# Second batch's scores and norms placed behind the first unit's products in an attention and MLP kernel

## The chip, the cores and the metric

One core of one Trainium2 chip runs the whole kernel. The metric is the device time of one execution in microseconds (us). Three runs of the kernel before took 824.13, 827.89 and 828.71 us; the median is 827.89 us.

## What is computed

The reference takes q, k and v of 4 batches, 8 heads, 576 positions and 64 features, and chains three blocks:

```python
out_up    = repeat(softmax_attention(mean4(q), mean4(k), mean4(v)), 4)   # 144 pooled positions
out_local = softmax(where(|i - j| < 4, q k^T / 8, -1e9)) v               # banded attention
x  = out_up + out_local                     # to (4, 576, 512)
u  = x + real(fft(fft(x, axis=1), axis=2))
ch = relu(layernorm(u) @ w_ch1) @ w_ch2     # 512 -> 2048 -> 512
y  = u + ch
out = (sigmoid(causal_conv5(y)) * (y @ w_val)) @ w_out
```

All inputs and outputs are float32. The weights reach the core as 64-bit floats and are turned into 32-bit ones by three integer operations on VectorE (DVE).

## The kernel before

The work has three kinds. **Attention and transform of a batch** (`attn_steps(b)`, L367): banded scores in five windows (`scores`, tile dS; then softmax into dP; `values`, tiles dPT, PT, dO), pooled attention (`lowres`, tiles sc, E, eT, po), then the transform: folds fs and fF, their fp16 halves FH and FL (L695 to L714), a first product over features (ab, L729) and a second over positions (pp, pq, pn, L754), added into X. **Twelve units** of 192 positions, three for each batch, `mlp_steps` (L907): layer norm `ln(b, j)` (L804, tiles uc, sq, st), eight groups of first products (`h_group`, tile ph), eight groups of second products (`c_group`, tile pc). Unit (0, 0) runs in 32-bit on the raw weights (`steps32`, L872, lines L885 and L896); the eleven others in three fp16 passes (L920, L938), for which the weights must first be split in halves (`conv_w`, L318). **The closing block** of a unit, `moe2_steps` (L961): taps of the convolution, `val` (L1017), `out_tile` (L1033). It needs the last weights, w_val and w_out (`weights3_steps`, L1095).

Weights arrive by `load_w(i)` (i = 0 to 7 the first matrix, 8 to 15 the second). `word_w(i)` (L283) makes 32-bit words of one slice, three DVE operations of 1024 columns, or twice three of 512 where the raw slice sits in two small buffers. `sumsq_w(i)` (L299) adds the squares of the slice on TensorE (PE, tile gram), and `w2_scale` takes the scale of the halves from that.

The order is set in two ways. Each step is put at a position on a line of time (`put`, `spread`; one unit is 1.0, unit n runs from n to n + 1, the start is negative) by the constants S_.. and P_.. at the head of the file; the steps are emitted in order of position. The framework then orders each engine's instructions when the kernel is built, by emission order, by priorities (`urgent`) and by its own model of the times; on the chip every engine runs its list in order. Two things bend this by hand: `behind(gate, f)` (L250) lets f's instructions be issued only after the gate instruction on the same engine, and the lists `gates` and `gates2` hold DVE instructions behind which the three operations of the weight words are placed, one entry for each operation until the last is left (L283 to L289). `load` chains the input transfers on SyncE's queue (SP) one behind the other in emission order until position S_CH = 0.9.

In the start, each word step of the second matrix is followed by its sum of squares (`w_in2`, S_W2 = -7.4 to -6.9); `ln(0, 0)` is put at S_N0 = -7.5, `ln(0, 1)` at S_N1 = -6.85, the second batch's scores at P_D[1] = -6.4 to -3.8. The first unit's products are put at 0 to 1. The scores of the second batch's first three windows use the two banks ps_h, which the first products use too (D1_H = 3).

Of the kernel before, what the change touches and what calls it, by code (L numbers as in the profile page):

```python
# [36 lines left out]
NSQ = 8  # L37
P_TAIL = ((0.08, 0.2), (-0.03, 0.03), (0.3, 0.5))
NORM_V = ((1, 0), (1, 1))
LN_V = ((0, 0), (1, 0), (2, 0), (3, 0))  # L40
CHAIN = True
S_CH = 0.9
S_LD = (-12.14, -11.9)
# [10 lines left out]
S_N0 = -7.5  # L54
S_W2 = (-7.4, -6.9)
S_C2 = (0.89, 0.94)
S_W3 = (0.945, 1.3)
P_D = {1: (-6.4, -3.8), 2: (1.6, 3.2), 3: (4.4, 6.0)}
P_E = {1: (0.2, 1.2), 2: (3.3, 4.5), 3: (6.1, 7.4)}
P_L = {1: 1.8, 2: 4.9, 3: 7.8}  # L60
EN_G = (1,)
SUM_V = (0,)
LN_PE = ((0, 0), (0, 1))
S_N1 = -6.85
XB_G = ((1, 1), (1, 3))
LASTV = True
U = {'F': 3000, 'N': 3000, 'X': 600, 'M': 0, 'V': 1000, 'O': 0, 'W': 0, 'R': 2000, 'S': 4000}
# [1 line left out]
P_VAL = (0.38, 0.65)  # L69
P_OUT = (1.12, 1.75)  # L70
P_LN = 0.3
D1_H = 3
LN_H = ()
LR0 = 0
TURN_V = False
# [42 lines left out]
def attn_moe_kernel(ctx, tc, qk_t, v_t, w1, w2, w_val, conv_t, w_out, c_feat, c_seq, c_band, c_eye, c_pool, out):  # L118
# [246 lines left out]
    st = {}  # L365

    def attn_steps(b):  # L367
# [60 lines left out]
        def dense(sp):  # L428
# [34 lines left out]
            def scores(r, e):  # L463

                q0, nq = QWIN[r]
                m = sc["band"][:, min(r, 1)].unsqueeze(1).to_broadcast([P, 4, P])
                pss = []
                for par in range(2):
                    ps = ps_h.tile([P, 4, P], F32, tag="h", name="dS") if first or (b == 1 and r < D1_H) else pst("dS", [P, 4, P])
                    behind(st[0]["seqed"].ins if b == 1 and r == 0 and par == 0 else None, lambda: T.matmul(  # L470
                        out=ps[0:nq], lhsT=sc["band"][:, 2, 0:nq], rhs=m, start=True, stop=False))
                    pss.append(ps)
                for a in range(4):
                    for par in range(2):
                        row = slice(par * 64, par * 64 + 64)
                        T.matmul(out=pss[par][0:nq, a], lhsT=d["X"][row, a, PAD + q0:PAD + q0 + nq],  # L476
                                 rhs=kT[a // 2][row, a % 2, WIN[r]:WIN[r] + 128], start=False, stop=(a == 3))
                mx = tiny.tile([P, 2, 4], F32, tag="dmx", name="dmx")
                su = tiny.tile([P, 2, 4], F32, tag="dsu", name="dsu")
                for par in range(2):  # L480
                    i = V.tensor_reduce(out=mx[0:nq, par], in_=pss[par][0:nq], axis=AX.X, op=ALU.max)  # L481
                if first:
                    gates.extend([i.ins] * (3 if r else 2))
                A.activation(out=mx[0:nq], in_=mx[0:nq], func=AF.Copy, scale=-SCALE)
                for par in range(2):
                    if first:
                        s_ = sp.tile([P, 4, P], F32, tag="S", name="dP", bufs=NS)
                    else:
                        s_ = mainp["S"].tile([P, 4, P], F32, tag="S", name="dP1")
                    for a in range(4):  # L490
                        to = {} if b in SUM_V else {"accum_out": su[0:nq, par, a:a + 1]}
                        A.activation(out=s_[0:nq, a], in_=pss[par][0:nq, a], func=AF.Exp, scale=SCALE,  # L492
                                     bias=mx[0:nq, par, a:a + 1], **to)
                    if b in SUM_V:
                        V.tensor_reduce(out=su[0:nq, par], in_=s_[0:nq], axis=AX.X, op=ALU.add)
                    e["s", par] = s_
                V.tensor_scalar(out=su[0:nq], in0=su[0:nq], scalar1=1e-9, scalar2=None, op0=ALU.add)
                V.reciprocal(out=su[0:nq], in_=su[0:nq])  # L498
                for par in range(2):
                    s_ = e["s", par][0:nq]  # L500
                    mul(V if b == 0 or (b, par) in NORM_V else G, s_, s_, su[0:nq, par].unsqueeze(2).to_broadcast([nq, 4, P]))
# [32 lines left out]
            if first:  # L534
                cuts = (0, WIN[2] + 128, S)
                ld = [lambda c=c, z=z, f=f: f(z, c, cuts[cuts.index(c) + 1])
                      for c in cuts[:2] for z in range(2) for f in (load_k, load_q)]
                for r in range(5):
                    ld.append(lambda r=r: load_vw(r))
                d["loads"] = [(1.0, f) for f in ld]  # L540
                for z in range(2):
                    for w in range(2):
                        steps.append((0.3, lambda z=z, w=w: pool_qk(z, w)))
                steps.append((0.3, lambda: pooled_v0(vw)))
            else:
                for z in range(2):
                    steps.append((0.1, lambda z=z: [load_k(z, 0, S), load_q(z, 0, S)]))
                steps.append((0.1, lambda: [load_vw(r) for r in range(5)]))

                def pool_v4(n):  # L550
                    x = [pr_t("v4", [QC, 512]) for _ in range(2)]
                    kc, h = n // 2, n % 2
                    for r in range(2):
                        load(out=x[r].rearrange("p (r c) -> p r c", r=2),
                             in_=v4[b, kc * QC:(kc + 1) * QC, 2 * r:2 * r + 2, h * 256:h * 256 + 256])
                    pooled_v([(kc, x)], n, h * 4, 4)
                v1 = [(0.1, lambda n=n: pool_v4(n)) for n in range(4)]
                for z in range(2):
                    for w in range(2):
                        steps.append((0.1, lambda z=z, w=w: pool_qk(z, w)))  # L560
            lr = []
            d["turned"] = len(steps)
            if b == 0:
# [129 lines left out]
        for sd in range(2):  # L693
            for c in range(2):
                def f(c=c, sd=sd):  # L695
                    X = d["X"]
                    s = prp.tile([P, S + 1], F32, tag="E", name="fs", bufs=3)
                    (V, V if b == 0 else G)[sd].tensor_tensor(
                        out=s, in0=X[:, c, PAD:PAD + S + 1], in1=X[:, c + 2, PAD:PAD + S + 1],
                        op=(ALU.add, ALU.subtract)[sd])  # L700
                    if b == 0:
                        F = mainp["tap"].tile([P, 2, HALF], F32, tag="tap", name="fF")
                    else:
                        F = prp.tile([P, 2, HALF], F32, tag="E", name="fF", bufs=3)
                    for e in range(2):
                        V.tensor_tensor(  # L706
                            out=F[:, e], in0=s[:, 0:HALF], in1=s[:, S:S - HALF:-1],
                            op=(ALU.add, ALU.subtract)[e])
                    h_ = d["FH"][:, c, sd, :, 0:HALF]
                    A.activation(out=h_, in_=F, func=AF.Copy, scale=d["sx"][:, 0:1])  # L710
                    i = stt(V, d["FL"][:, c, sd, :, 0:HALF], F, d["sx"][:, 0:1], h_, ALU.mult, ALU.subtract)
                    if b == 0:
                        gates2.extend([i.ins] * 2)
                steps.append((2.1, f))  # L714

        @step(0.0)
# [87 lines left out]
    def ln(b, j):  # L804
# [5 lines left out]
        def colsum(t, src):  # L810
            if (b, j) in LN_PE:
                ps = pst("st", [P, UT])
                for c in range(4):
                    T.matmul(out=ps, lhsT=ones, rhs=src[:, c], start=(c == 0), stop=(c == 3))
                return ps
            add(eng, t[:, 0:2], src[:, 0:2], src[:, 2:4])
            add(eng, t[:, 0], t[:, 0], t[:, 1])
            ps = ps_h.tile([P, UT], F32, tag="h", name="st") if (b, j) in LN_H else pst("st", [P, UT])
            T.matmul(out=ps, lhsT=ones, rhs=t[:, 0], start=True, stop=True)
            return ps  # L820
# [51 lines left out]
    def steps32():  # L872
# [4 lines left out]
        def h_group(g):  # L877
# [3 lines left out]
            for e in range(2):  # L881
                m = 2 * g + e
                for kc in range(4):
                    o = (m % 8) * 128
                    T.matmul(out=ps[:, e], lhsT=W[kc * 2 + m // 8 + 1][:, o:o + 128], rhs=u()[:, kc, :],  # L885
                             start=(kc == 0), stop=(kc == 3))
            A.activation(out=hs[-1][:, g % 2], in_=ps, func=AF.Relu)

        def c_group(g):
# [193 lines left out]
    def w_in2(i):  # L1083
        if i >= 11:
            load_w(i)
        w_in(i)

    def w_in(i):
        word_w(i)
# [36 lines left out]
    put(S_L1, lambda: [load_w(i) for i in range(8)])  # L1126
    put(S_K, load_consts2)
    put(S_W1[1], lambda: urgent(w1_scale, "S"))
    put(S_W2[1], lambda: urgent(w2_scale, "S"))
    put(S_LW2, lambda: [load_w(i) for i in range(8, 11)])  # L1130
    put(S_CH, lambda: chain.update(on=False))
    for steps, p in ((st[0]["loads"], S_LD), (a0[:c0], S_T0), (a0[c0:c1], S_S0), (a0[c1:], S_F0)):
# [26 lines left out]
    for n, (b, j) in enumerate(units):  # L1159
        main = mlp_steps(b, j)  # L1160
        spread([(1.0, f) for f in main], n, n + 1)
        if j + 1 < UPB:
            put(n + P_LN if n else S_N1, lambda b=b, j=j: urgent(lambda: ln(b, j + 1), "N"))
        ps = [P_TAP, P_VAL, P_OUT]
        if n == B * UPB - 2:
            ps[1:] = [tuple(1 + x for x in P_TAIL[1]), tuple(1 + x for x in P_TAIL[2])]
        if n == B * UPB - 1:
# [52 lines left out]
```

## Time and profile before

| | |
|---|---|
| Median of 3 runs | 827.89 us (824.13 to 828.71) |
| The profiled execution's own time | 826.63 us |
| Its span in the trace | 824.8 us |
| PE busy | 753.9 us (91%) |
| Weight loads into PE (PEld) busy | 651.7 us (79%) |
| DVE busy | 481.0 us (58%) |
| ScalarE (ACT) busy | 397.4 us (48%) |
| GpSimd (POOL) busy | 189.1 us (23%) |
| Granted PE clock, mean | 0.935 of 2.4 GHz |
| Read and written in HBM | 45.37 MB and 9.45 MB |

Times in the profile are from the start of the span. A tile's name without its number names all its buffers: W is any slice of the weights, X a batch's activations. A busy PE is not PE at its peak: matmuls overlap, so the pace is read from the distance between starts. The granted clock is 1.0 at 2.4 GHz and 0.5 at 1.2 GHz.

### The profile page before, as it was taken

How to read it: one execution, taken by the hardware profiler on the slowest of the kernel's cores; microseconds unless marked ns; L12 is line 12 of the kernel's file. 1: busy time of each engine (PE TensorE's matmuls, PEld its weight loads, DVE VectorE, ACT ScalarE, POOL GpSimd, SP SyncE). 2: the span in 40 equal slices, each digit the busy share in tenths (PEclk: the TensorE clock that was granted, in tenths of full speed). 3: DMA queues.
4: the chain of work that ended last, by engine and by line, in shares of the span. 5: the costliest groups of instructions: out<-in, count | busy, mean ns of one | idle time of the engine just before them, and what ended most of it. 6: DMA issues, size and time to landing. Idle time of an engine off the chain costs nothing.

```text
span 824.8 us, 17392 instructions
## 1 busy us (share of the span) xinstructions
PE 753.9 (91%) x7234; PEld 651.7 (79%) x7234; DVE 481.0 (58%) x942; ACT 397.4 (48%) x1156; POOL 189.1 (23%) x192
## 2 busy tenths in 40 slices
PE   5887687998979999998989999989989999999996
PEld 2666555887869898886869888978779998989894
DVE  5895968657878575336596732237765526252224
ACT  2573222545674366776562664575552516151512
POOL 0000000015243124363061341341232305040300
PEclk9875666899989999998999999999999999999998
DMA  9753540244202100122021000010110000000001
GB/s 323 312 188 127 182 149 0 86 128 146 77 2 87 59 16 26 35 80 81 29 72 59 1 15 22 9 43 2 53 59 4 14 1 14 14 15 2 26 2 39
DMA packets 25849, 53.58 MB, mean 65 GB/s; under 512 B 1989, under 2 KB 11973, under 8 KB 24746
## 3 DMA queue, kind: packets, MB, share of 16 engines
q1 hardware_dynamic: 25770, 52.47, 18.8%
q8 instruction: 57, 0.93, 0.5%
q14 instruction: 22, 0.18, 0.1%
HBM read 45.37 MB, written 9.45 MB: 66 GB/s over the span
## 4 chain that ended last, share of the span: by engine, by line
PE 65%; DVE 19%; DMA 5%; issue 4%; ACT 4%; POOL 3%; SPq 1%; POOLq 0%; DVEq 0%; ACTq 0%
PE pc L938 18%; PE ph L920 17%; PE val L1017 5%; PE out L1033 4%; DVE W L155 4%; PE dS L476 4%; DVE fF L706 2%; PE dO L522 2%; DVE FL L155 2%; PE ab L729 2%; PE po L650 2%; DMA v<-in_v_dram 2%; PE dPT L511 1%; DMA raw<-in_moe_w_val_dram 1%; DMA raw<-in_moe_w_out_dram 1%
## 5 line engine op out<-in xcount | busy, mean ns | idle before, releaser
L938 PE MATMUL pc<-hh,W 128*128 128x192 f16 x1408 | 199.1, 249 | 1.7 <-ACT hh L924 1.7
L920 PE MATMUL ph<-uh,W 128*128 128x192 f16 x1408 | 195.9, 247 | 0.3 <-ACT uh L849 0.3
L938 PEld LDWEIGHTS <-W 128*128 128x128 f16 x2112 | 178.4, 99 | 16.2 <-issue 11.2
L920 PEld LDWEIGHTS <-W 128*128 128x128 f16 x2112 | 176.0, 98 | 9.0 <-issue 5.7
L938 PE MATMUL pc<-hl,W 128*128 128x192 f16 x704 | 173.8, 250 | 4.3 <-DVE hl L155 4.3
L920 PE MATMUL ph<-ul,W 128*128 128x192 f16 x704 | 173.7, 247 | 1.4 <-DVE ul L850 1.4
L155 DVE SCALAR_TENSOR_TENSOR hl<-ph,hh 128x384 f16<-128x384 f32 x88 | 48.4, 552 | 116.9 <-ACT hh L924 116.9
L161 POOL TENSOR_TENSOR W<-W,tap 128x768 f32<-128x768 f32 x40 | 73.3, 1833 | 164.1 <-ACT tap L996 159.9
L924 ACT ACTIVATE hh<-ph 128x384 f16<-128x384 f32 x88 | 42.2, 484 | 80.7 <-PE ph L920 80.3
L996 ACT ACTIVATE tap<-X,cw 128x192 f32<-128x192 f32 x180 | 66.5, 445 | 8.2 <-DMA out_dram<-osb 4.8
L492 ACT ACTIVATE dP<-dS,dmx 112x128 f32<-112x128 f32 (+2 forms) x160 | 53.2, 372 | 10.2 <-PE dPT L511 9.8
L1017 PE MATMUL val<-yy,W 128*128 128x192 f16 x576 | 54.4, 249 | 2.0 <-DVE yy L155 1.2
L1017 PEld LDWEIGHTS <-W 128*128 128x128 f16 x576 | 49.0, 99 | 5.1 <-issue 3.6
L1033 PE MATMUL out<-W,gh 128*128 128x512 f16 x144 | 46.6, 383 | 0.0
L158 POOL TENSOR_TENSOR dP<-dP,dsu 112x512 f32<-112x512 f32 (+2 forms) x20 | 22.5, 1148 | 72.1 <-DVE dsu L498 57.8
L481 DVE TENSOR_REDUCE dmx<-dS 112x4 f32<-112x512 f32 (+2 forms) x40 | 27.2, 684 | 16.5 <-PE dS L476 16.2
L1033 PE MATMUL out<-W,gl 128*128 128x512 f16 x72 | 27.6, 383 | 2.1 <-DVE gl L155 2.1
L729 PE MATMUL ab<-feat,FH 128*97 128x128 f16 (+5 forms) x192 | 22.0, 244 | 8.1 <-ACT FH L710 7.8
L155 DVE SCALAR_TENSOR_TENSOR W<-W,W 128x1024 int32<-128x1024 int32 x24 | 28.6, 1214 | 0.0
L516 ACT ACTIVATE PT<-dPT 128x448 f32<-128x448 f32 (+2 forms) x40 | 21.7, 558 | 13.3 <-PE dPT L511 13.3
L729 PE MATMUL ab<-feat,FL 128*97 128x128 f16 (+5 forms) x96 | 18.3, 248 | 10.1 <-DVE FL L155 10.0
L511 PE MATMUL dPT<-eye,dP 112*128 112x112 f32 (+2 forms) x160 | 25.2, 294 | 1.6 <-ACT base L654 1.6
(207 smaller groups left out, 1357.8 us busy)
## 6 DMA issues: line engine op xcount, KB each, us to landing
W<-in_moe_w_ch_dram SPq DMA_DIRECT2D x12, 1024.0 KB
X<-in_qk_dram SPq DMA_DIRECT2D x8, 576.0 KB
out_dram<-osb SPq DMA_DIRECT2D x18, 256.0 KB
v<-in_v_dram SPq DMA_DIRECT2D x24, 144.0 KB
vwkv<-in_v_dram SPq DMA_DIRECT2D x12, 256.0 KB
dx<-X SPq DMA_DIRECT2D x4, 576.0 KB
dr<-dx SPq DMA_DIRECT2D x4, 576.0 KB
X<-dr SPq DMA_DIRECT2D x4, 576.0 KB
```

What stands on the lines that cost most here:

```text
L155: return eng.scalar_tensor_tensor(out=out, in0=in0, scalar=scalar, in1=in1, op0=op0, op1=op1)
L161: return eng.tensor_tensor(out=out, in0=a, in1=b, op=ALU.add)
L476: T.matmul(out=pss[par][0:nq, a], lhsT=d["X"][row, a, PAD + q0:PAD + q0 + nq], rhs=kT[a // 2][row, a % 2, WIN[r]:WIN[r] + 128], start=Fals ...
L492: A.activation(out=s_[0:nq, a], in_=pss[par][0:nq, a], func=AF.Exp, scale=SCALE, bias=mx[0:nq, par, a:a + 1], **to)
L511: T.transpose(out=ps[:, a, 0:nq], in_=e["s", par][0:nq, a], identity=eye[0:nq, 0:nq])
L729: T.matmul(out=ps[0:n, c0:c1], lhsT=d[x][:, c, sd, e, n0:n0 + n], rhs=feat[:, w, c, c0:c1], start=(t == 0), stop=(t == 5),)
L920: T.matmul(out=ps[:, e], lhsT=w1_ap(pw, kc, 2 * g + e), rhs=uh[px][:, kc, :], start=(t == 0), stop=(t == 11))
L924: A.activation(out=h_, in_=ps, func=AF.Relu)
L938: T.matmul(out=ps[m // 2][:, m % 2], lhsT=w2_ap(pw, kk, m), rhs=x[px][:, e, :], start=(kk == 0 and (pw, px) == (0, 0) and m % 2 == 0), sto ...
L996: A.activation(out=g[:, c], in_=X[:, c, c0:c0 + UT], func=AF.Copy, scale=cw[:, c, t:t + 1])
L1017: T.matmul(out=ps[:, e], lhsT=wv_ap(pw, kc, 2 * mh + e), rhs=m_["y"][px][:, kc, :], start=(t == 0), stop=(t == 11))
L1033: T.matmul(out=ps, lhsT=(gh, gl)[px][:, kc, t * 128:(t + 1) * 128], rhs=wo_ap(pw, kc), start=(n == 0), stop=(n == 11))
```

## The change

It moves steps on the line of time, and changes what some of them wait for.

- The word steps of the second matrix no longer carry their sums of squares; those are put at 0.2 to 0.44, and `w2_scale` at 0.44.
- `gates2` loses the eight entries of the transform's folds (FL). Left are six of the first product's halves (AL), four of the second's (DS), and the first norm (u).
- The scores of the second batch move from -6.4..-3.8 to 0.02..0.94, with their loads of v; those of the first window, and the sums of `ln(0, 1)`, are placed behind `ph`, the last matmul of the first unit's first group. They use the banks t, no longer ps_h. The pooling of k goes behind the scores.
- `ln(0, 1)` moves to 0.1, `ln(0, 2)` from 1.3 to 0.9, its adds from POOL to DVE.
- The second batch's pooled attention and transform move from 0.2..1.2 to 0.96..1.85, its first norm from 1.8 to 2.1; the third batch's scores begin at 2.0 instead of 1.6.
- The last weights move from 0.945..1.3 to 1.02..1.6; the first unit's taps from 0.95..1.35 to 1.4..1.75, its val from 1.38..1.65 to 1.8..2.0, its out from 2.12..2.75 to 2.3..2.75.

```diff
-LN_V = ((0, 0), (1, 0), (2, 0), (3, 0))
+LN_V = ((0, 0), (0, 2), (1, 0), (2, 0), (3, 0))
...
-S_W3 = (0.945, 1.3)
-P_D = {1: (-6.4, -3.8), 2: (1.6, 3.2), 3: (4.4, 6.0)}
-P_E = {1: (0.2, 1.2), 2: (3.3, 4.5), 3: (6.1, 7.4)}
-P_L = {1: 1.8, 2: 4.9, 3: 7.8}
+S_W3 = (1.02, 1.6)
+S_G2 = (0.2, 0.44)
+P_D = {1: (0.02, 0.94), 2: (2.0, 3.2), 3: (4.4, 6.0)}
+P_E = {1: (0.96, 1.85), 2: (3.3, 4.5), 3: (6.1, 7.4)}
+P_L = {1: 2.1, 2: 4.9, 3: 7.8}
+P_T0 = ((0.4, 0.75), (0.8, 1.0), (1.3, 1.75))
...
-S_N1 = -6.85
+S_N1 = 0.1
+S_N2 = 0.9
...
-D1_H = 3
+D1_H = 0
...
-                    behind(st[0]["seqed"].ins if b == 1 and r == 0 and par == 0 else None, lambda: T.matmul(
+                    behind(st[0]["ph"].ins if b == 1 and r == 0 else None, lambda: T.matmul(
...
-                    for w in range(2):
+                    for w in range(1 if b == 1 else 2):
                         steps.append((0.1, lambda z=z, w=w: pool_qk(z, w)))
+                if b == 1:
+                    v1 += [(0.1, lambda z=z: pool_qk(z, 1)) for z in range(2)]
...
                     i = stt(V, d["FL"][:, c, sd, :, 0:HALF], F, d["sx"][:, 0:1], h_, ALU.mult, ALU.subtract)
-                    if b == 0:
-                        gates2.extend([i.ins] * 2)
...
-                    T.matmul(out=ps, lhsT=ones, rhs=src[:, c], start=(c == 0), stop=(c == 3))
+                    behind(st[0]["ph"].ins if j else None, lambda c=c: T.matmul(
+                        out=ps, lhsT=ones, rhs=src[:, c], start=(c == 0), stop=(c == 3)))
...
+            if g == 0:
+                st[0]["ph"] = i
             A.activation(out=hs[-1][:, g % 2], in_=ps, func=AF.Relu)
...
     def w_in2(i):
         if i >= 11:
             load_w(i)
-        w_in(i)
+        word_w(i)
...
-    put(S_W2[1], lambda: urgent(w2_scale, "S"))
+    spread([(1.0, lambda i=i: sumsq_w(i, "w2", i == 8, i == 15)) for i in range(8, 16)], *S_G2)
+    put(S_G2[1], lambda: urgent(w2_scale, "S"))
...
-            put(n + P_LN if n else S_N1, lambda b=b, j=j: urgent(lambda: ln(b, j + 1), "N"))
+            put((n + P_LN if n > 1 else S_N2) if n else S_N1, lambda b=b, j=j: urgent(lambda: ln(b, j + 1), "N"))
         ps = [P_TAP, P_VAL, P_OUT]
+        if n == 0:
+            ps = list(P_T0)
```

## Rows read from the trace of the kernel before

**Rows 1.** The page, span in 40 slices of 20.6 us: PE busy, granted clock

```profile
PE   5887687998979999998989999989989999999996
...
PEclk9875666899989999998999999999999999999998
```

**Rows 2.** Timeline, all engines, 75 to 125 us: start, length, instruction

```profile
86.18 0.69 DVE L261 TENSOR_SCALAR W<-W 128x1024 int32<-128x1024 int32 x1
...
89.59 2.35 DVE L155 SCALAR_TENSOR_TENSOR W<-W,W 128x1024 int32<-128x1024 int32 x2
...
91.86 0.82 DVE L155 SCALAR_TENSOR_TENSOR FL<-fF,s_x,FH 128x578 f16<-128x578 f32 x1
```

**Rows 3.** Timeline, 105 to 147 us

```profile
107.97 1.06 PE L306 MATMUL gram<-W 128*128 128x128 bf16 x8
...
112.70 1.22 DVE L155 SCALAR_TENSOR_TENSOR W<-W,W 128x1024 int32<-128x1024 int32 x1
113.83 1.56 DVE L161 TENSOR_TENSOR X<-X,DS 128x289 f32<-128x289 f32 x4
...
123.72 2.93 PE L814 MATMUL st<-sq,ones 128*128 128x192 f32 x8
...
128.73 0.95 DVE L824 TENSOR_TENSOR uc<-X,st 128x768 f32<-128x768 f32 x1
...
131.24 0.96 DVE L158 TENSOR_TENSOR u<-uc,r 128x768 f32<-128x768 f32 x1
...
132.23 0.84 ACT L826 ACTIVATE sq<-uc 128x768 f32<-128x768 f32 x1 [5.93 <-DVE u L158]
...
133.99 5.13 DVE L529 TENSOR_REDUCE qkT<-X 128x288 f32<-128x1152 f32 x4
...
143.56 1.76 SPq L176 DMA_DIRECT2D vwkv<-in_v_dram  x4
...
145.92 1.04 PE L306 MATMUL gram<-W 128*128 128x128 bf16 x8 [1.12 <-DVE W L155]
```

**Rows 4.** Timeline of PE, 146.6 to 161 us

```profile
146.75 5.09 PE L885 MATMUL ph<-u,W 128*128 128x192 f32 x16
...
153.66 2.87 PE L885 MATMUL ph<-u,W 128*128 128x192 f32 x16 [0.58 <-ACT h L887]
...
157.16 0.40 PE L470 MATMUL dS<-bandb 128*112 128x512 bf16 x1
...
158.54 0.99 PE L522 MATMUL dO<-PT,vwkv 128*64 128x112 f32 x16
159.46 0.42 PE L470 MATMUL dS<-bandb 128*112 128x512 bf16 x1
```

**Rows 5.** Stages, 92.7 to 109 us: length, PE, PEld, DVE, ACT, POOL busy, clock, DMA

```profile
92.70:95.50 2.80, 2.77 (x26) 2.77 (x27) 2.80 (x4) 0.00 (x0) 0.00 (x0) 0.50 0.21 27
...
97.80:100.00 2.20, 2.17 (x31) 2.00 (x32) 2.10 (x5) 0.44 (x2) 0.46 (x4) 1.00 1.03 419
...
106.00:109.00 3.00, 3.00 (x18) 2.23 (x17) 1.80 (x5) 0.88 (x2) 0.00 (x0) 0.50 0.78 229
```

**Rows 6.** Stages, first and second unit, the columns of rows 5

```profile
146.65:220.30 73.65, 69.41 (x453) 61.45 (x452) 48.39 (x105) 39.57 (x116) 16.76 (x18) 0.94 0.35 107
220.30:277.00 56.70, 51.48 (x553) 46.02 (x550) 44.69 (x75) 30.85 (x78) 19.29 (x20) 0.94 0.20 63
```

**Rows 7.** Groups of DVE, 146.65 to 220.3 us: busy, mean ns, idle before

```profile
L155 DVE SCALAR_TENSOR_TENSOR W<-raw,W 128x512 int32<-128x512 int32 x15 | 11.5, 766 | 0.3
...
L261 DVE TENSOR_SCALAR W<-raw 128x512 int32<-128x512 int32 x8 | 4.4, 552 | 14.6 <-DMA raw<-in_moe_w_out_dram 8.8 <-DMA raw<-in_moe_w_val_dram 5.8
```

**Rows 8.** Timeline of DVE, 186 to 237 us

```profile
215.82 1.26 DVE L155 SCALAR_TENSOR_TENSOR W<-W,s_w 128x1024 f16<-128x1024 f32 x1
...
235.29 3.01 DVE L155 SCALAR_TENSOR_TENSOR W<-W,s_w 128x1024 f16<-128x1024 f32 x1 [1.00 <-ACT W L321]
```

**Rows 9.** Timeline of POOL, 229 to 240 us

```profile
235.42 1.80 POOL L161 TENSOR_TENSOR tap<-tap 128x768 f32<-128x768 f32 x1
```

More of the change, by code (lines that the diff above doesn't have):

```diff
@@ L884, in h_group @@
                     o = (m % 8) * 128
-                    T.matmul(out=ps[:, e], lhsT=W[kc * 2 + m // 8 + 1][:, o:o + 128], rhs=u()[:, kc, :],
-                             start=(kc == 0), stop=(kc == 3))
+                    i = T.matmul(out=ps[:, e], lhsT=W[kc * 2 + m // 8 + 1][:, o:o + 128], rhs=u()[:, kc, :],
+                                 start=(kc == 0), stop=(kc == 3))
+            if g == 0:
+                st[0]["ph"] = i
             A.activation(out=hs[-1][:, g % 2], in_=ps, func=AF.Relu)
```

## The prediction

> **What bounds the kernel now.** I read the page's slices first [rows 1]. In the first seven slices, some 144 us, PE is busy 5 to 8 tenths and its clock falls to half; from the eighth on it is busy 8 to 9 tenths or more at a clock near full, to the end. So the kernel is a start that waits on chains, and then a run bound by PE. A change in the start is worth what it brings the run forward, less the PE work that it puts into the run.
>
> The timeline around the turn [rows 3, 4] shows why the run begins where it does. The first unit's norm u ends at 131.24 + 0.96 = 132.20 us, and its products need only that and words long done; yet the first stands at 146.75. Ahead of it in PE's list are scores, transposes and values of the second batch, the second norm's sums, and the sums of squares of the weights; the last of these, at 145.92, has itself waited 1.12 us for DVE's words, and DVE had spent 5.13 us from 133.99 on pooling the second batch. The products wait 14.55 us for work that they don't need.
>
> The same neighbours sit inside the chain to u. The last add into X ends at 113.83 + 1.56 = 115.39; u is done 16.81 us later [rows 3].
>
> **The change, part by part.** Negative is earlier.
>
> (a) Folds. Weight words run between the folds' halves: 0.69 us at 86.18 and 2.35 at 89.59, right ahead of the last half at 91.86 [rows 2]. Without their entries in the list they go behind the first product's halves. Between 0 (another wait ends last) and their 3.0 us I take -2.5, as the last half also needs ACT's copy.
>
> (b) The second transform product. A sum of squares of 1.06 us stands in PE's list at 107.97, and a word of 1.22 us at 112.70 delays the adds into X [rows 3]. The first goes; the second is replaced by operations of half the size, since the list now reaches the slice in two pieces there. Between 0 and -2.3 I take -1.5.
>
> (c) The fill that is lost. PE runs at 0.50 from 92.70 and at 1.00 from 97.80, with sums of squares in the gap between the transform's products; at 106.00 it is back at 0.50 [rows 5]. Without the fill the 2.17 us of products in the stage from 97.80 could take twice that. Between 0 and +2.2 I take +1.1.
>
> (d) The norm's chain without neighbours. From the sums at 123.72 to u's end are 8.48 us, of which 0.95 at 128.73 belongs to the next norm: 7.5. Ahead of that stand a subtraction (0.95, the same operation), a square (0.84 at 132.23), and the last two sums on X (a quarter of the 2.93 for eight, 0.7) [rows 3]. With half a us for hand-overs that is 10.5 instead of 16.81: -6.3. If words or scores slip in again it is half, -3.1; more than the 6.8 that lies without the hand-overs it can't be.
>
> (e) From u to the first product: -14.5 of the 14.55 [rows 3, 4]. The fence holds the first window's scores and the next norm's sums behind the first group; the other windows come after the first in the same order, and the sums of squares are emitted later.
>
> Sum of (a) to (e): -23.7 us; the first product at about 123.
>
> (f) What joins the run. Three windows' scores: a tile takes 1.38 us from 157.16 to 158.54, six make 8.3. One set of values takes 0.92 (158.54 to 159.46), its transposes, half as many instructions on wider tiles, I set at 1.0 [rows 4]; bounds half and double that. Of 64 sums of squares 56 ran early: eight take 1.06 at half clock [rows 3, 5], 0.53 at full, so seven times that, 3.7. The second norm's sixteen sums have the form of the products, sixteen in 2.87 [rows 4]: 2.9. Together +16.8. This is paid in full, since the run has next to no free PE.
>
> (g) What else moves. The words' operations behind u (20 of 30) take at most 20 times 1.22, 24 us of DVE [rows 3]; the second products need the first of them only after eight groups of first products, each a little under 2.87 us [rows 4], some 21 us, and the last some 18 us after that. So they are hidden; without the cover each us late is a us. The second batch's loads of v (five, then eight pooled ones) move back on SP with their scores, and POOL's pooled sums of v with them; four of them left at 143.56 [rows 3], and behind them in the chain stand no weights of the first unit. The values that wait for them can be passed by products: 0. Pooling, second norm, scores come after the words on DVE, again beside products. The last weights, the pooled attention and the transform go from the first unit to the second and third; PE pays them at either place: 0, with both ends in the rivals. The third norm's adds go from POOL to DVE, under 2 us there (two pairs, each less than two of the 0.95): 0 beside PE.
>
> Net: -23.7 + 16.8 = -6.9. The sum is made on the profiled execution, 826.63 us: 819.7. The median of the runs shown lies 1.3 higher, and I forecast the new one at **820.5**.
>
> **Rivals.**
>
> *The gain is eaten in the start and by the clock* (no change). The chain to u gets only half of (d), +3.2; the lost fill costs the whole of (c), +1.1; and the moved work runs like the first unit's stage, busy 69.41 of 73.65 us at 0.94 [rows 6], so 16.8 becomes 19.0: +2.2. 819.7 + 6.5 = 826.2. For it: PE will stand nearly idle through the norm, and the first sixteen products took 5.09 us against 2.87 later [rows 4]. Against: they began at half clock before, too. The Trainium skill, "TensorE: Matmul & The Clock Gate", section "Loop structure matters more than you think", says that matmuls keep the high clock only if nothing long is waited for between them, which speaks against taking fill out of the start; the trace agrees at 92.70 and 97.80, and by that rule the forecast would end near this rival.
>
> *DVE becomes the bound of the second unit* (slower). In 220.30 to 277.00 it is busy 44.69 of 56.70 us, PE 51.48 [rows 6]. The last weights' words, 11.5 + 4.4 us, ran in the first unit [rows 7] and go here: 60.6, 9.1 over PE. Half of that may leave with the folds that move on to the third unit. And POOL's adds slow it: a conversion of 1.26 us took 3.01 beside a tap add of 1.80 [rows 8, 9]; with four tap adds in the stage that is 4 times 1.75, 7.0. The most is 16, I set it at 13: 833. It decides from the point where DVE's work in the stage passes PE's, since each product waits for a DVE half. Against it: the positions spread this work over 0.6 of a unit. The Trainium skill, "SBUF — State Buffer", section "SBUF: two separate sides", says that DVE with two SBUF inputs and GpSimd share ports that one holds for a whole instruction; the 3.01 agrees, being the sum of the other two within 0.05.
>
> *The retuned middle recovers losses* (faster still). The two stages hold 4.2 and 5.2 us without PE work, and at 0.94 some 4.2 and 3.1 more [rows 6]. Half of that is 8.4: 811.3. Nothing in the rows says that later positions do this.
>
> *The change doesn't do what it says.* The lists are ordered by a model at build time; the products may keep some of the queue ahead. Then (e) and (f) both fall away: 819.7 + 14.5 - 16.8 is 817.4 if all of it stays ahead, but with DVE's words now later in front of them the sums could cost the 14.5 again, 831.9.
>
> **How the numbers follow.** Forecast 0.47, recovered middle 0.12, eaten gain 0.21, DVE bound 0.16, not as said 0.04, half of it to no change and half to slower. A difference under 0.5%, 4.1 us, can't be told from none. Faster takes the forecast and the recovered middle, 0.59; within 0.5% the eaten gain and half of the last, 0.23; slower the DVE bound and the other half, 0.18. The range from 811 to 832 reaches the recovered middle and the eaten gain, and stops short of the worst of the DVE bound.
>
> **What would show it.** In the profile after: no words between the folds' halves, last half near 89.4; the last add into X near 112.5; u about 10.5 us later; the first product within 0.3 us of u, near 123; gram and second-batch dS only after it; in the first unit's stage PE busy 9 tenths or more; in the second, DVE below PE. Wrong if the first product comes after 130, if PE has holes of more than 8 us between the first and the third unit, or if the second products wait for words.

## The result, and the profile after

Beside four runs of the kernel before (median 827.72 us), four of the changed kernel have a median of **813.23 us** (811.25 to 814.91): a ratio of 0.9846, 95% interval 0.981 to 0.9883. Forecast were 820.5, within 811 to 832. In a second measurement, reported with the experiments, the ratio is 0.9901 (0.9862 to 0.994), some 8 us of 826.43. The ratios leave out executions over 1.5% above the fastest of their kernel, one of the six of the second measurement (829.70 us) and the profiled one of e6 among them. The direction is right; the gain forecast, 7.2 us, lies a little under the second measurement and at half of the first.

The page's slices of the changed kernel, PE busy and granted clock, to set beside [rows 1]:

```profile
PE   5896759999789998999989999989899999999996
...
PEclk9858569999999999999999999989999999999999
```

The weak start has shrunk from seven slices to six. The low slice that remains behind it, the eleventh, is the second unit.

The timeline of the changed kernel's start, all engines (start, length, instruction, and in brackets the engine's idle time before it and what ended it), to set beside [rows 2 to 4]:

```profile
83.17 2.27 DVE L158 SCALAR_TENSOR_TENSOR FL<-fF,s_x,FH 128x578 f16<-128x578 f32 x3
...
87.03 0.82 DVE L158 SCALAR_TENSOR_TENSOR FL<-fF,s_x,FH 128x578 f16<-128x578 f32 x1 [0.85 <-ACT FH L715]
...
107.05 1.55 DVE L164 TENSOR_TENSOR X<-X,DS 128x289 f32<-128x289 f32 x4
...
111.18 2.93 PE L817 MATMUL st<-sq,ones 128*128 128x192 f32 x8 [1.92 <-ACT sq L830]
...
117.48 0.96 DVE L161 TENSOR_TENSOR u<-uc,r 128x768 f32<-128x768 f32 x1
118.49 4.97 PE L889 MATMUL ph<-u,W 128*128 128x192 f32 x16 [4.39 <-DVE u L161]
```

No word stands between the folds' halves. From the last add into X (107.05 + 1.55 = 108.60) to the end of u (118.44) are 9.84 us instead of 16.81, and the first product follows u by 0.05 us instead of 14.55. It starts at 118.49, **28.26 us earlier**.

What of that reaches the end is read by cutting both spans at the first product. Stages of the kernel before, up to it and behind it (length, PE, PEld, DVE, ACT and POOL busy, clock, DMA):

```profile
80.00:146.75 66.75, 45.20 (x283) 34.86 (x284) 55.61 (x93) 18.43 (x63) 2.17 (x8) 0.65 0.34 119
146.75:824.80 678.05, 645.53 (x6547) 573.16 (x6545) 366.43 (x725) 340.90 (x961) 186.33 (x175) 0.98 0.12 39
```

The same cut of the changed kernel, then its first and second unit (as [rows 6]):

```profile
80.00:118.49 38.49, 22.59 (x153) 17.79 (x153) 26.61 (x54) 7.89 (x15) 2.34 (x7) 0.63 0.33 104
118.49:813.00 694.51, 658.80 (x6675) 584.88 (x6675) 388.91 (x765) 350.75 (x1008) 182.19 (x172) 0.98 0.13 43
...
118.40:190.50 72.10, 72.01 (x517) 65.88 (x517) 59.66 (x102) 39.62 (x122) 1.05 (x2) 0.97 0.26 92
190.50:246.00 55.50, 45.13 (x468) 39.11 (x467) 43.81 (x90) 32.87 (x98) 23.51 (x22) 0.97 0.30 90
```

Behind the first product the run is 694.51 us long instead of 678.05: it has 128 matmuls more, 13.27 us more of PE's busy time, and 3.19 us more of its idle time (35.71 against 32.52). So 28.26 are gained, 16.46 paid back, 11.8 left (the profiled execution is the slowest of the four; by the medians it is 14.5). The first unit's stage is full; the second has 10.4 us without PE work, 4.66 of them in one wait for an hl:

```profile
204.61 2.98 DVE L158 SCALAR_TENSOR_TENSOR W<-raw,W 128x512 int32<-128x512 int32 x1
207.01 0.47 ACT L930 ACTIVATE hh<-ph 128x384 f16<-128x384 f32 x1
207.52 0.55 DVE L158 SCALAR_TENSOR_TENSOR hl<-ph,hh 128x384 f16<-128x384 f32 x1
...
208.12 0.32 PE L944 MATMUL pc<-hl,W 128*128 128x192 f16 x1 [4.66 <-DVE hl L158]
```

DVE was at a weight word until then, which took 2.98 us where its like took 0.68 at 211.21; POOL was at additions from 203.78 on. But ACT, too, ended the hh that this hl needs only at 207.48, behind other work of its own. Which of the two held it can't be told apart.

### The profile page after: what moved, and what is told of

It is laid out like the page before. It is cut to its first block, busy times and chain, and to the rows that moved or that the text cites. A ratio compares the mean times of both kernels' runs of the same rounds, so it can differ in the third digit from the quotient of the medians.

```text
span 813.0 us, 17403 instructions
## 1 busy us (share of the span) xinstructions
PE 744.6 (92%) x7234; PEld 646.3 (79%) x7234; DVE 476.8 (59%) x946; ACT 397.3 (49%) x1156; POOL 185.2 (23%) x188
## 4 chain that ended last, share of the span: by engine, by line
PE 68%; DVE 19%; DMA 5%; ACT 3%; issue 2%; POOL 1%; SPq 1%; ACTq 0%; POOLq 0%; DVEq 0%
PE pc L944 17%; PE ph L926 16%; PE dS L479 4%; PE val L1023 4%; PE out L1039 4%; DVE W L158 4%; PE ph L889 3%; PE dO L525 3%; DVE fF L711 2%; PE po L655 2%; DMA raw<-in_moe_w_val_dram 2%; PE ab L732 2%; PE pc L902 2%; DVE FL L158 2%; PE dPT L514 1%
## 5 line engine op out<-in xcount | busy, mean ns | idle before, releaser
L926 PE MATMUL ph<-uh,W 128*128 128x192 f16 x1408 | 199.2, 248 | 0.3 <-ACT uh L853 0.3
L926 PEld LDWEIGHTS <-W 128*128 128x128 f16 x2112 | 178.3, 99 | 10.3 <-issue 6.2
L164 POOL TENSOR_TENSOR W<-W,tap 128x768 f32<-128x768 f32 x40 | 75.1, 1878 | 152.2 <-ACT tap L1002 122.9
L732 PEld LDWEIGHTS <-FH 128*97 128x97 f16 (+1 forms) x192 | 19.7, 149 | 11.2 <-ACT FH L715 7.7
L889 PE MATMUL ph<-u,W 128*128 128x192 f32 x128 | 24.5, 350 | 4.4 <-DVE u L161 4.4
L889 PEld LDWEIGHTS ph<-u,W 128*128 128x128 f32 x128 | 22.8, 206 | 5.2 <-DVE u L161 4.9
```

The source lines that it names most:

```text
L164: return eng.tensor_tensor(out=out, in0=a, in1=b, op=ALU.add)
L732: T.matmul(out=ps[0:n, c0:c1], lhsT=d[x][:, c, sd, e, n0:n0 + n], rhs=feat[:, w, c, c0:c1], start=(t == 0), stop=(t == 5),)
L889: i = T.matmul(out=ps[:, e], lhsT=W[kc * 2 + m // 8 + 1][:, o:o + 128], rhs=u()[:, kc, :], start=(kc == 0), stop=(kc == 3))
L926: T.matmul(out=ps[:, e], lhsT=w1_ap(pw, kc, 2 * g + e), rhs=uh[px][:, kc, :], start=(t == 0), stop=(t == 11))
```

## The experiments

Two theories stood at the outset: **theory 1**, the gain is the earlier first product less the PE work moved behind it; **rival A**, it comes from the rearranged middle. After the first four runs a **theory 2** was added: an earlier start is worth its time only while each unit's u is ready when the unit before it ends.

All runs in one table. "Behind" is the span less the start of the first product; busy and idle are PE's in it. "Work" is that busy time with every stretch multiplied by the clock granted in it: an estimate, from the trace, of what it would be at full clock. "uh late" is the start of the third unit's uh less the end of the second unit's products (the start of the last add of pc into X): negative is in time. The ratio is to the kernel before, run beside each group; the changed kernel itself stood only in the first measurement and beside e8 to e10, so a difference to it in other groups carries the spread of both ratios. Of e6's profile no stages are given.

```
run                  ratio (95%)              first   behind   busy   work   idle   uh late
kernel before        1                        146.75  678.05  645.5  631.9  32.5   -13.3
changed kernel       0.9846 (0.981,  0.9883)  118.49  694.51  658.8  645.1  35.7   -22.4
e0 changed again     0.9901 (0.9862, 0.994)   124.76  692.44  657.9  645.0  34.6   -21.9
e1 scores back       1.0019 (0.9976, 1.0063)  130.89  693.21  647.9  633.7  45.4   (2nd: +19)
e2 sums back         0.9999 (0.9959, 1.0039)  125.46  700.04  665.5  648.5  34.6    -7.9
e3 second norm back  0.9952 (0.9917, 0.9987)  129.44  692.16  655.1  644.5  37.0   -22.0
e4 gates back        0.9920 (0.9887, 0.9953)  126.36  690.84  655.3  643.1  35.6   -22.2
e5 middle back       1.0113 (1.0009, 1.0216)  118.76  715.54  666.8  645.8  48.8   +31.5
e6 late u            0.9965 (0.9927, 1.0003)  132.93
e7 few squares       0.9841 (0.9807, 0.9875)  122.50  685.50  652.4  641.0  33.1   -23.0
e8 third norm back   1.0114 (1.0076, 1.0152)  120.61  712.59  661.3  645.4  51.3   +33.1
e9 outputs back      0.9976 (0.9941, 1.0011)  128.33  699.67  660.1  647.3  39.6   -21.2
e10 middle alone     1.0091 (1.0058, 1.0125)  144.80  683.90  644.6  630.9  39.3   -63.2
e11 third norm 1.1   0.9961 (0.9929, 0.9994)  123.78  699.12  661.3  645.8  37.9    +5.1
```

**e0, the changed kernel again.** No edit.

> The changed kernel itself, unaltered, on the chip of the three runs beside it, since the runs of the kernel before spread over 14 us there. Every theory: 0.981 to 0.988 of the kernel before (about 12 us less).

0.9901, outside the expected band by 0.002; the interval overlaps the first one's. Behind the first product it differs from the first profile by 2.07 us only; the first product comes 6.27 us later. Where from is in the last section. A variant is therefore judged by both parts, the start of the first product and the length behind it; in these two profiles the second repeats better. It has a spread of its own: behind the third unit, where both run the same 5065 matmuls, they take 507.80 and 504.80 us.

**e5, the middle put back.**

```diff
-LN_V = ((0, 0), (0, 2), (1, 0), (2, 0), (3, 0))
+LN_V = ((0, 0), (1, 0), (2, 0), (3, 0))
...
-S_W3 = (1.02, 1.6)
+S_W3 = (0.945, 1.3)
...
-S_N2 = 0.9
+S_N2 = 1.3
...
```

(P_D[2], P_L[1] and the first unit's outputs go back to their places too. P_E[1] goes to 0.94 to 1.75, hardly moved, as its old place, 0.2 to 1.2, begins before the scores end.)

> Only the places of the steps in the units behind the first are put back as before (third unit's sums on TensorE again, third matrix's scale at 0.945 to 1.3, the second batch's windows from 1.6 for the third batch's scores, the values' steps from 0.94 to 1.75, the first unit's outputs at their old places, the second unit's sums at 1.3); the start stays as changed. Theory 1 (the gain is the earlier first product less the TensorE work moved behind it): -2 to +3 us against the changed kernel (811 to 816). Rival A (the start's gain is eaten by the work moved behind it, and the gain in time comes from these places): +8 us or more (821 and up).

Theory 1 falls here: with the start kept, at 118.76, the kernel is slower than before by 1.1%. The run behind is 21.03 us longer than the changed kernel's. The stage of e5 behind its second unit, and of the changed kernel behind its own (columns as above):

```profile
250.60:284.00 33.40, 22.24 (x150) 16.57 (x151) 28.31 (x66) 16.80 (x33) 10.58 (x8) 0.69 0.21 63
```

```profile
247.40:284.00 36.60, 35.48 (x407) 31.59 (x406) 26.69 (x62) 22.99 (x52) 14.38 (x13) 1.00 0.19 58
```

In the one PE runs 407 matmuls, the third unit's among them; in the other 150, with 11 us idle and the clock at 0.69, as it has only the second batch's pieces to run.

**e8, only the third unit's norm put back** (LN_V and S_N2 of the diff above: the engine of its adds, and its place).

> Only the third unit's norm is put back: its place from 0.9 to 1.3, and its sums of the features from VectorE's adds to where they were before; all else stays as changed. Theory 2 (an earlier start is worth its time only as far as each following unit's u is ready when the unit before ends; with the middle put back, the third unit's u came 32 us after the second unit's end, by the rows of that run, where the changed kernel had it 22 us ahead): most of the 21 us lost behind the first product by the run with the whole middle put back is this, so +14 to +22 us against the changed kernel (827 to 835). Theory 1 (only the start and the TensorE work behind it count): -2 to +2 us (811 to 815).

The same as e5: ratio 1.0114, 18.1 us longer behind. The timeline of e8, the third unit's norm on DVE:

```profile
257.71 0.95 DVE L828 TENSOR_TENSOR uc<-X,st 128x768 f32<-128x768 f32 x1 [0.27 <-PE st L823]
...
281.64 2.44 DVE L161 TENSOR_TENSOR uc<-uc,r 128x768 f32<-128x768 f32 x1
```

and of the changed kernel:

```profile
199.21 0.94 DVE L828 TENSOR_TENSOR uc<-X,st 128x768 f32<-128x768 f32 x1
...
224.02 0.94 DVE L161 TENSOR_TENSOR uc<-uc,r 128x768 f32<-128x768 f32 x1
```

From this first row to uh are 26 us in both, between other work of DVE. With the second unit ending at 251.0 and 247.4, the one is 33.1 us late (uh at 284.1), the other has 22.4 to spare. The old place, 1.3, was in time in the kernel before (uh at 264.2, the unit's end at 277.5), where the second batch's scores had been done ahead. PE's idle time behind the first product is 15.5 to 16.7 us longer than in the two profiles of the changed kernel, most of what was lost. So what the middle is needed for is above all this norm; whether by its place or by the engine of its adds, which went back together, e8 doesn't tell.

**e11, the third norm at 1.1.**

```diff
-S_N2 = 0.9
+S_N2 = 1.1
```

> The third unit's norm is asked for at 1.1 in place of 0.9 units (its sums stay on VectorE), a place between the changed kernel's and the one that cost 16 us or more. Theory 2 says that what counts is whether its u is there when the second unit ends (it had 22 us to spare): if it still is, VectorE is freer in the second unit, where TensorE waited 4.7 us for one hl, and the end moves by -4 to +1 us; if it is not, each us that u is late is a us of the end. Theory 1: -1 to +1 us.

uh comes 5.1 us late and the run behind is 4.6 to 6.7 us longer than in the two profiles of the changed kernel. That is theory 2's number (the interval of the ratio overlaps e0's), but not its wait. The stages of PE from the end of the second unit to the third unit's first product, then to the third unit's end, in e11 (length, PE busy, clock, DMA):

```profile
253.21:260.21 7.00, 6.78 (x45) 1.00 0.06 20
253.21:316.20 62.99, 60.13 (x639) 1.00 0.17 53
```

and the second of them in the changed kernel:

```profile
247.36:305.20 57.84, 56.72 (x617) 1.00 0.18 58
```

While uh is late, PE is busy with other pieces. The third unit takes 5.2 us longer, 3.4 of them in 22 matmuls that ran elsewhere before and 1.7 idle; the fourth, with 17 matmuls fewer, gives back 0.9 only. In e8, 33.1 us late cost 18.1 to 20.2: there the hole was only in part filled, and PE is idle for 15.9 of the third unit's 101.0 us. So what a given lateness costs is not settled; that a late third u costs, e5 and e8 show.

**e10, the middle alone,** on the kernel before: all places of the middle of the change, none of the start.

> The kernel before with the changed kernel's places for the middle alone (third unit's norm at 0.9 with its sums on VectorE, third matrix, the first unit's outputs, the second batch's values, the third batch's scores); start as before. Theory 2 (the middle only keeps an earlier start from being lost): -3 to +4 us against the kernel before (ratio 0.996 to 1.005). Rival A (the gain is the middle's own): -8 us or more (ratio under 0.990).

Rival A falls: 0.9% slower. The run behind is 5.85 us longer than before: 6.8 us more of idle time, 0.9 less of busy time. The longest new wait is one of 6.07 us for an hh in the second unit. Start alone +1.1%, middle alone +0.9%, both -1.0 to -1.5%: the parts don't add up, they need each other.

**e9, first unit's outputs and third matrix put back.**

```diff
-S_W3 = (1.02, 1.6)
+S_W3 = (0.945, 1.3)
...
-        if n == 0:
-            ps = list(P_T0)
```

> Only the places of the first unit's output steps and of the third matrix's steps are put back (taps from -0.05, values from 0.38, outputs from 1.12 units after the unit, third matrix from 0.945 to 1.3); the third unit's norm stays as changed. Theory 2 (the third unit's norm is what counts of the middle): -2 to +4 us against the changed kernel (811 to 817). Rival (the outputs' steps hold VectorE while the second and third units need it): +8 us or more (821 and up).

Behind the first product 5.2 to 7.2 us are lost: above theory 2's +4, below the rival's +8. The third norm was in time, so this is another, smaller cost. It comes late: at the fourth unit's end the run is level with the changed kernel's (272.4 us from the first product, against 272.0 and 273.4), and the fifth unit then takes 65.7 us instead of 60.4 and 60.1, with some 65 matmuls more. The fourth had 88 fewer but ran at a clock of 0.94 instead of 0.97 to 0.98, with a wait of 3.4 us for POOL. The edit put back the last weights as well as the outputs; which of the two costs it is not shown.

**e1, the scores put back.**

```diff
-P_D = {1: (0.02, 0.94), 2: (2.0, 3.2), 3: (4.4, 6.0)}
-D1_H = 0
+P_D = {1: (-6.4, -3.8), 2: (2.0, 3.2), 3: (4.4, 6.0)}
+D1_H = 3
...
-                    behind(st[0]["ph"].ins if b == 1 and r == 0 else None, lambda: T.matmul(
+                    behind(st[0]["seqed"].ins if b == 1 and r == 0 and par == 0 else None, lambda: T.matmul(
```

> The second batch's scores go back to their old place ahead of the first unit (steps at -6.4 to -3.8 units, three windows on the held PSUM pool, the fence on their first matmul as it was); all else stays as changed. Theory 1 (TensorE is the bound from the first product on, so the time is the start of the first product plus the TensorE work behind it): the first product starts about 9 us later (8.3 us of score matmuls and whatever they wait for stand in front of it again) and the run behind it has about 8.3 us less to do, so the end moves by 0 to +4 us (813 to 817 against the changed kernel's 813). Rival A (the gain lies in the fill: the scores, queued behind, run in TensorE's idle time): the end moves by +8 us or more, since the first product is late and nothing is given back.

Neither number is met (ratio 1.0019). The timeline of PE in e1:

```profile
118.69 1.12 PE L479 MATMUL dS<-X 64*112 64x128 f32 x8
129.71 0.61 PE L309 MATMUL gram<-W 128*128 128x128 bf16 x4 [9.89 <-DVE W L158]
130.89 4.35 PE L889 MATMUL ph<-u,W 128*128 128x192 f32 x16 [0.57 <-ACT dP L495]
...
218.18 0.48 PE L926 MATMUL ph<-uh,W 128*128 128x192 f16 x2 [11.51 <-ACT uh L853]
```

u was done at 120.60; a sum of squares that waited 9.89 us for a word holds the products until 130.89. This is the queue of [rows 3] again, in 10.3 of its 14.55 us. Behind the first product 84 matmuls and 10.94 us of busy time are gone, near the 10.2 that the prediction priced for the scores with their transposes and values; but idle time is 9.64 up, since now the second unit's u is 19 us late (the first unit ends at 197.9, uh starts at 217.3). What theory 1 gives back, theory 2 takes.

**e2, the squares put back.** `w_in2` calls `w_in` again; `w2_scale` at S_W2[1].

> The squares of the second matrix's last eight slices are again taken as each slice comes in, and the scale of the second matrix is asked for where it was; all else stays as changed. Theory 1 (the order decides only what stands in front of the first product): the 64 squares of about 0.066 us are 4 us of TensorE work that leaves the run behind the first product and lies ahead of it; ahead of it TensorE has idle time, so the end moves by -2 to +2 us. Rival (the squares wait for their slices' words on VectorE and hold the queue in front of the first product): the first product starts 4 to 15 us later and the end comes out +4 to +15 us (817 to 828).

The edit did not do what it was meant to: 6675 matmuls stand behind the first product as before, so the build placed the squares behind it all the same. It says nothing on the squares' place. Yet the order behind changed. The first unit runs 124 matmuls fewer, and at the third unit's end the run is 14 us ahead (172.5 us from the first product, against 186.7 and 187.6). The fourth and fifth units take more than that back: 163.3 us instead of 145.7 and 145.9, at a clock of 0.95 instead of 0.97 to 0.98, with PE idle 11.9 us in them instead of 6.8 and 7.1. In all the run behind is 5.5 to 7.6 us longer, and half of the longer busy time is the clock (work is up by 3.5 of 6.7 to 7.6).

**e3, the second norm put back.** S_N1 = -6.85, no fence on its sums.

> Only the second unit's norm goes back to its old place (asked for at -6.85 units, without the fence behind the first product); all else stays as changed. The prediction's term (d), -6.3 us, says that the first unit's norm runs faster without it: so u comes 4 to 7 us later, TensorE has 2.9 us of sums less behind the first product, and the end moves by +1 to +4 us against the changed kernel. Rival (the sums, in TensorE's idle time ahead of the first product, cost the first norm nothing): -3 to 0 us.

From the last add into X to u 11.21 us, against 9.84 and 10.26 in the two profiles of the changed kernel: the second norm costs the first 1.0 to 1.4 us, so term (d) is mostly not its doing. Busy time behind falls by 2.7 to 3.7 us. That this is near the 2.9 priced is chance: only 8 of the second norm's 16 sums left the run, 1.4 by that price, and work falls by 0.5; the rest is the clock. The end can't be told apart from e0's: the first fold stood at 84.06 in this profile, 3.8 to 5.8 us later than in those, ahead of the edit.

**e4, the gates put back:** the folds' entries in `gates2`.

> Only the folds of the first batch are again in the list of the instructions behind which the second set of weights' words may go, so that words stand between them; all else stays as changed. The prediction's term (a), -2.5 us: the last FL comes 2.0 to 3.0 us later after the first fold than in the changed kernel (9.60 us in its profile from the first fold's start to the last FL's end) and the end moves by +1 to +3 us. Rival (the words only change places with others on VectorE, and the first product stays): -1 to +1 us.

From the first fold's start to the last FL's end 12.14 us, as in the kernel before (80.54 to 92.68), against 9.60: term (a) is 2.54 us, exactly its size before. With the words 20 more squares ran ahead of the first product, so not all else stayed. The end is within the noise of e0.

**e6, a late u:** 26 multiplications by one on the norm's tile.

> 26 dependent VectorE passes over the norm's small tile are put in front of the first unit's u (a multiplication by one each, about 0.4 us), which delays u by about 10 us and changes nothing else. Theory 1 (every us of the first product's start is a us of the end): +8 to +11 us (821 to 824). Rival (there is slack behind the start, by which a later start is partly made up as TensorE's waits for VectorE in the second unit shrink; TensorE stood idle 10.4 us there): +2 to +6 us.

The timeline of e6:

```profile
124.24 7.64 DVE L847 TENSOR_SCALAR r<-r 128x192 f32<-128x192 f32 x26
131.92 0.96 DVE L161 TENSOR_TENSOR u<-uc,r 128x768 f32<-128x768 f32 x1
```

A pass costs 0.29 us, not 0.4, so u is 7.64 us late by it. The ratio is 0.0064 above e0's (5.3 us) and 0.0119 above the first measurement's (9.8 us); their mean is 7.6. That fits a late start that is a late end, us for us, but the intervals are too wide to tell this from half of it.

**e7, few squares.**

```diff
-        for c in range(8):
+        n = 1 if key == "w2" else 8
+        for c in range(n):
...
+        V.tensor_scalar(out=f, in0=f, scalar1=8.0, scalar2=None, op0=ALU.mult)
```

> The second matrix's sum of squares takes one block of 128 columns of each slice in place of eight and multiplies the result by eight, so the scale is of a part of the matrix only; 56 matmuls of about 0.066 us leave TensorE's run. Theory 1 and the prediction's term (f) price them at 3.7 us behind the first product: -2.5 to -4 us against the changed kernel. Theory 2 (the run is as long as its work only while each u is in time, and TensorE has idle time in the second unit that takes them in): -1 to +1 us.

The run behind is 6.9 to 9.0 us shorter, more than either theory, though only 39 matmuls left it (17 of the 56 had run ahead of the first product). Cut by units it is theory 1's: the first unit, full in all three profiles, takes 69.40 us instead of 73.31 and 74.34, 3.9 to 4.9 less, and the second and third are as long as there. The rest lies behind the third unit, where the same 5065 matmuls take 502.60 us instead of 507.80 and 504.80, at a clock of 0.99 instead of 0.98; the squares are not in that. By the ratios the kernel is 5 us under e0 and level with the first measurement. PE work taken out of a full stage shortens it.

## Why the prediction was right

Term by term, in the first profile and in e0's (us; negative is earlier):

```
term                                  forecast   first profile    e0
first fold's start                        0         -2.29        -0.23
(a) folds                                -2.5       -2.54        -2.55
(b)+(c) second product, lost fill        -0.4       -1.96        +1.83
(d) norm's chain                         -6.3       -6.97        -6.55
(e) u to the first product              -14.5      -14.50       -14.49
first product                           -23.7      -28.26       -21.99
(f) PE busy behind it                   +16.8      +13.27       +12.32
(g) the rest: PE idle behind it           0         +3.19        +2.07
sum, span                                -6.9      -11.8         -7.6
```

(The column (b)+(c) is the last FL's end to the last add into X: 22.71 us before, 20.75 and 24.54 after.)

**The start was read right.** (a), (d) and (e) lie within 0.7 us of their forecasts in both profiles, and e1 shows (e) coming back when the scores do. The sum of (b) and (c) came out within their bounds of -2.3 and +2.2 each time, on either side of nothing, with the clock (below). (d) passed the 6.8 that was called its most by 0.17 in the first profile. In (d) the neighbour that mattered most was not the second norm, 1.0 to 1.4 us by e3, but the scores: in e1 the way from the last add into X to u takes 13.66 us, 3.4 to 3.8 more. The remaining 2 or so, squares and words, were not tested singly.

**The work moved behind was priced high.** (f) was 3.5 to 4.5 us too much as busy time, 1.3 of it because 36 squares moved and not 56: of both matrices' squares 120 stood ahead of the first product before, and 84 still do. PE is idle 2 to 3 us more behind it, which (g) had at nothing. That the whole came so near in e0 is these two set against each other and against a start 1.7 us later than forecast; the first profile's further 4.2 us come from its start. (The forecast itself is not quite its sum: 819.7 and 1.3 make 821.0, and no reason is given for 820.5.)

**Of the signs of being wrong none came.** The first product stands before 130 in both profiles, the first unit's second products wait for no word, and the longest hole of PE up to the third unit is 4.66 us. That hole, in the second unit, comes nearest: words stood ahead of its hl.

**The step that was right only by luck is (g).** It took the moved norm, outputs and last weights as neutral "at either place". Their sum is near nothing, but the parts tested are not: with the third norm put back the run behind is 18 to 20 us longer and the kernel slower than before (e8); the place of the outputs and last weights is worth 5 to 7 (e9). The rival "the retuned middle recovers losses" asked whether the middle adds a gain; the question to ask was what an earlier start does to due times that don't move with it. The norm's margin could be read in the trace of before: uh at 264.2, needed at 277.5, 13 us. A start that comes 24 us earlier, with the second batch's work now between, uses that up: in e8 the same place is 33 us late.

The rival **DVE bound of the second unit** was wrong in size: DVE is 43.81 us busy there, PE 45.13, and the stage lasts 55.50 instead of 56.70. What it described, DVE slowed beside POOL's adds, may be in the rows as the one wait of 4.66 us for an hl, not as a bound. The rival **by the clock** had its mechanism in the start, 4.2 us between two runs of one program, but not behind it, where the clock is 0.98 as before. The Trainium skill, "TensorE: Matmul & The Clock Gate", section "Loop structure matters more than you think", speaks against taking fill out. These traces don't decide it: of the squares that filled the transform's products (32 from 95.5 to 109 us before) 16 still ran there in both profiles, and the second product ran mostly at full clock in the first profile and mostly at half clock in e0.

## What to carry to other kernels

Cut the span where the bound changes hands, and count on each side busy and idle time of the engine that bounds the second part; a change then shows as an earlier cut, added work and added waiting, each of which can be checked. Before pricing a step as "neutral at either place", read how long ahead of its use it is done: an earlier start shortens that margin for everything that doesn't move along, and a missed margin can cost more than the net gain (18 to 20 us in e8, against 8 to 12). Where several moves were made together, undo the smallest one alone; here one norm decided the sign. And before a busy time is set against a price, count the matmuls that moved and look at the clock: runs with the same 6675 matmuls behind the first product had PE busy for 657.9 to 666.8 us.

## What was not expected of the hardware

The same program has starts that differ by 6 us, and the granted clock is where they part. Stages of PE in the first profile of the changed kernel (length, PE busy, clock, DMA):

```profile
40.00:50.00 10.00, 9.89 (x54) 0.50 0.34 103
50.00:60.00 10.00, 10.00 (x51) 0.50 0.62 215
60.00:70.00 10.00, 9.36 (x89) 0.76 0.66 218
...
88.00:98.00 10.00, 7.91 (x63) 0.50 0.36 93
98.00:106.00 8.00, 6.49 (x53) 0.94 0.68 252
```

and in e0, the same kernel:

```profile
40.00:50.00 10.00, 9.08 (x63) 0.73 0.34 109
50.00:60.00 10.00, 7.68 (x61) 0.78 0.60 208
60.00:70.00 10.00, 10.00 (x69) 0.50 0.63 214
...
88.00:98.00 10.00, 6.36 (x63) 0.75 0.34 97
98.00:106.00 8.00, 6.59 (x37) 0.62 0.78 262
```

The full clock falls on the second half of the first batch's attention in the one and on its middle in the other; the first fold starts at 78.25 and 80.31. From 98 to 106 the one runs 53 matmuls at 0.94, the other 37 at 0.62, and from the last FL to u they need 30.59 and 34.80 us. In e3, whose edit comes later, the clock is at 0.50 or 0.51 in every stage from 40 to 80 us, and its first fold starts at 84.06. What decides which of these a run gets, no run here shows. The first product was forecast at about 123; the one profile lies 4.5 us ahead of that, the other 1.8 behind. A start of this kind can't be judged from one profile to better than this.
